# Top-32 attention and a hard-swish feed-forward in one kernel: attention in steps of two units, feed-forward blocks of 256 tokens

## The chip, the cores and the metric

The kernel runs on one core of one Trainium2 chip. The metric is the device time of one execution in microseconds (us). The engines are TensorE (PE in the rows; PEld is its weight load), VectorE (DVE), ScalarE (ACT), GpSimd (POOL) and SyncE (SP), which issues the DMAs here.

## The reference

`q`, `k` and `v` have 8 batches, 8 heads, 576 rows and 64 columns, in float32. For each head, scores are `q @ k.T / 8`. In each row the 32 largest scores stay, the others become -1e9; then a softmax with 1e-9 added to its denominator, and a product with `v`. The heads of a token, side by side, are a row of 512, so there are 4608 rows `x`. The feed-forward is

```
h = x @ w_in                      # 512 x 2048
g = h * clip(h + 3, 0, 6) / 6
out = g @ w_out                   # 2048 x 512
```

The two weight matrices arrive as 64-bit floats and are turned into float32 on the chip.

## The kernel before, in words

**Units.** A pair is two heads of one batch (four pairs in a batch, `Pair`). Its 576 rows of q and k are loaded, transposed on TensorE and copied out of PSUM once (`Pair.transpose`, L171 to L185). A unit is one pair and one tile of 128 query rows (`Unit`); the last 64 rows of both heads of a pair share a rest unit with half the work for DVE. A batch has 16 full and 4 rest units, and 160 units run in one loop (L448).

**A unit's steps.** `scores` (L198): matmuls into the PSUM tile `big`, two copies by ACT into `sc`. `top` (L228): four rounds, each a MAX8 for every row tile and, but for the last round, a MATCH_REPLACE8; this is nearly all of DVE's work. `exp` (L240): three small POOL instructions, then two passes of ACT over each row tile and an add on POOL. `weights` (L263): a reciprocal on DVE and a scaling of each row tile on POOL. `transpose` (L271): nine transposes (six for a rest unit) into `big`, one ACT copy to `eT`. `values` (L282): 20 matmul calls into a PSUM tile `pv`, and an ACT copy for two units together (L418).

**Buffers in PSUM.** `big` has one buffer of four banks, and scores, transposes and the transposes of q and k all go through it. `h`, `acc` and `pv` share four buffers of one bank (`ps_w`), and so does `f` of the weight conversion.

**Feed-forward.** When all four pairs of a token tile have their values, `queue` appends a `feed_forward` generator (L300). It takes 128 tokens in 16 pieces: 8 pieces for h (two pieces fill one `h` tile of four 128-column results, then ACT makes `g`, and a `gate` on DVE finishes it two pieces later), and 8 for the second product (L328). The loop asks for a number of pieces at set places (`piece`, L361); for a full unit four when `left`, the pieces still queued, is at least 8, and else three; for a rest unit two or one. After the loop all that is left runs (L503).

**Order.** The program is scheduled by hand: each engine's queue holds its instructions in the order in which the program lists them. In iteration n the loop lists the scores of unit n+1, the four rounds of unit n, `exp` of unit n-1, and weights, transposes and values of unit n-2. While n is under 8 the lag is one unit: weights, transposes and values are those of unit n-1 and come after round 2. Between the rounds stand four conversions of a weight chunk per unit (`convert`, L95), 32 in all, each with two ACT, two DVE and two POOL instructions.

Of the kernel before, what the change touches and what calls it, by code (L numbers as in the profile page):

```python
# [15 lines left out]
TOP_K = 32  # L16
# [11 lines left out]
def kernel(  # L28
# [26 lines left out]
    ldpool = pool("ld", 2)  # L55
# [10 lines left out]
    ps_w = pool("ps_w", 4, space=PSUM)  # L66
# [12 lines left out]

    ring = []  # L80
    for i in range(2 * NHP):
        vm = const([P, 2, J, D], f"vm{i}")
        vr = const([P, 2, D], f"vr{i}")
        nc.gpsimd.memset(vr[:], 0.0)
        ring.append((vm, vr))

    def big():

        return ps_big.tile([P, 4 * 512], F32, tag="big", name="big")
# [5 lines left out]
    def convert(dst, src):  # L95
# [10 lines left out]
        f = ps_w.tile([P, WC], F32, tag="w", name="f")  # L106
# [3 lines left out]
        nc.scalar.activation(f[:], lo, AF.Copy, bias=2.0, scale=2.0**-51)  # L110
# [7 lines left out]
            out=yu, in0=hi, scalar=0x80000000, in1=f[:].bitcast(U32),  # L118
# [18 lines left out]
    class Pair:  # L137


        def __init__(self, b, hp):  # L140
            self.b, self.hp = b, hp
            self.vm, self.vr = ring[(b * NHP + hp) % len(ring)]

        def load(self):
            h0 = 2 * self.hp
            self.rest = ldpool.tile([P, 2, D], F32, tag="rest", name="rest")
            for i, (name, src) in enumerate((("kin", k), ("qin", q))):
                t = ldpool.tile([P, J, 2, D], F32, tag=name, name=name)
                setattr(self, name, t)
                for hh in range(2):  # L150
                    nc.sync.dma_start(
                        t[:, :, hh, :],
                        src[self.b, h0 + hh, 0:JP, :].rearrange("(p j) d -> p j d", j=J),
                    )
                nc.sync.dma_start(
                    self.rest[i * R : (i + 1) * R, :, :],
# [14 lines left out]
        def transpose(self):  # L171
            kq = kqpool.tile([P, 2, S], F32, tag="kq", name="kq")
            self.kT, self.qT = kq[:, 0, :], kq[:, 1, :]
            ps = big()
            for i, src in enumerate((self.kin, self.qin)):
                for j in range(J):
                    rows = src[:, j, :, :].rearrange("p h d -> p (h d)")
                    c0 = i * JP + j * P
                    nc.tensor.transpose(ps[:, c0 : c0 + P], rows, ident[:])  # L179
            c0 = 2 * JP  # L180
            nc.tensor.transpose(
                ps[:, c0 : c0 + P], self.rest[:].rearrange("p h d -> p (h d)"), ident[:]
            )
            nc.scalar.copy(kq[:, :, 0:JP], ps[:, 0:c0].rearrange("p (t s) -> p t s", t=2))
            nc.scalar.copy(kq[:, :, JP:S], ps[:, c0 : c0 + P].rearrange("p (t s) -> p t s", t=2))  # L185

    class Unit:
# [5 lines left out]
        def __init__(self, pair, qt):  # L193
            self.pair, self.qt = pair, qt
            self.rest = qt == J
            self.nt = 1 if self.rest else 2

        def scores(self):  # L198
            pr, q0 = self.pair, self.qt * P
            ps = big()  # L200
            qs = slice(q0, min(q0 + P, S))
            heads = [slice(0, D), slice(D, P)]
            sc = self.sc = scpool.tile([P, 2 * (S + R)], F32, tag="sc", name="sc")
            if self.rest:
                for s0, s1 in ((0, JP), (JP, S)):
                    for d in heads:
                        nc.tensor.matmul(ps[d, s0:s1], pr.qT[d, qs], pr.kT[d, s0:s1])  # L207
                nc.gpsimd.memset(sc[:, S : S + R], 0.0)
                nc.scalar.copy(sc[:, 0:S], ps[:, 0:S])
                return  # L210
            banks = ps[:].rearrange("p (n s) -> p n s", s=512)
            for i, (s0, s1) in enumerate(((0, JP), (JP, S))):
                for hh, d in enumerate(heads):
                    nc.tensor.matmul(banks[:, 2 * i + hh, 0 : s1 - s0], pr.qT[d, qs], pr.kT[d, s0:s1])  # L214
            nc.scalar.copy(  # L215
                sc[:].rearrange("p (h s) -> p h s", h=2)[:, :, 0:JP], banks[:, 0:2, 0:JP]
            )
            nc.scalar.copy(  # L218
                sc[:, JP : JP + 2 * R].rearrange("p (h r) -> p h r", h=2), banks[:, 2:4, 0:R]
            )  # L220

        def begin(self):
            self.m = mpool.tile([P, 2, TOP_K], F32, tag="m", name="m")
            self.wk = wkpool.tile([P, 2, S], F32, tag="wk", name="wk")
            self.row = [self.sc[:, t * S : (t + 1) * S] for t in range(self.nt)]
            self.cur = list(self.row)

        def top(self, r):  # L228

            for t in range(self.nt):  # L230
# [9 lines left out]
        def exp(self):  # L240

            nt = self.nt
            kth = mpool.tile([P, 2], F32, tag="kth", name="kth")
            shift = mpool.tile([P, 2], F32, tag="shift", name="shift")
            self.den = mpool.tile([P, 2], F32, tag="den", name="den")
            last = self.m[:, 0:nt, TOP_K - 1]
            nc.gpsimd.tensor_scalar_mul(kth[:, 0:nt], last, -1.0)  # L247
            nc.gpsimd.tensor_tensor(shift[:, 0:nt], last, self.m[:, 0:nt, 0], ALU.subtract)
            nc.gpsimd.tensor_scalar_mul(shift[:, 0:nt], shift[:, 0:nt], scale)
            for t in range(nt):  # L250
                nc.scalar.activation(  # L251
                    self.row[t], self.row[t], AF.Prelu, bias=kth[:, t : t + 1], scale=1.0,
                    alpha=STEEP,
                )
            for t in range(nt):
                nc.scalar.activation(  # L256
# [283 lines left out]
```

## Time and profile before

| | us |
|---|---|
| median of 3 runs | 1802.66 (1802.39 to 1805.76) |
| the profiled execution, its own time | 1803.79 |
| span of its instructions | 1802.0 |
| PE busy | 1638.0 (91%) |
| DVE busy | 1548.2 (86%) |
| ACT busy | 968.7 (54%) |
| POOL busy | 408.3 (23%) |
| mean granted clock of TensorE | 0.970 |

The profile has 40 equal slices of 45 us. PE is at 3 to 8 tenths in the first five and at 9 in nearly all others; DVE is at 5 to 9 in the first eight, at 8 or 9 later, and at 2 and 0 in the last two. A matmul in float32 shows up as two instructions, so the counts of matmuls are twice those of the calls.

### The profile page before, as it was taken

The numbers are of one execution on the slowest core, as the hardware profiler recorded it, in microseconds if no ns is written. First come the engines' busy times: TensorE is split into PE (matmuls) and PEld (weight loads), VectorE is DVE, ScalarE is ACT, GpSimd is POOL, SyncE is SP. The second block draws the span as 40 slices with busy tenths as digits, with TensorE's granted clock in tenths as the row PEclk, the third lists the DMA queues.
The fourth block names the chain that finished last, engine by engine and source line by source line (L and its number), as shares of the span: only waits on it lengthen the run. The fifth ranks groups of instructions, "written<-read, shape, count | busy, mean of one in ns | idle before, by whom it ended". The sixth has DMA issues, their size and how long they took to land.

```text
span 1802.0 us, 31081 instructions
## 1 busy us (share of the span) xinstructions
PE 1638.0 (91%) x11872; PEld 1198.3 (66%) x11872; DVE 1548.2 (86%) x3249; ACT 968.7 (54%) x1717; POOL 408.3 (23%) x1038
## 2 busy tenths in 40 slices
PE   3356798989999999999999999999999999999999
PEld 2244666667677777777777766677677666777775
DVE  5767788989899899999999988999899888999920
ACT  5444555555655655555655555556555555555530
POOL 3544122222122112212121221211121122122110
PEclk9867899999999999999999999999999999999999
DMA  6431100011001110111011100011011010000000
GB/s 189 135 114 55 46 7 14 15 26 46 7 7 46 27 27 7 27 46 27 7 27 27 46 7 7 26 46 27 7 27 27 26 27 7 7 7 7 7 7 12
DMA packets 101140, 56.53 MB, mean 31 GB/s; under 512 B 84096, under 2 KB 92288, under 8 KB 100992
## 3 DMA queue, kind: packets, MB, share of 16 engines
q1 hardware_dynamic: 100992, 54.55, 10.9%
q8 instruction: 94, 1.54, 0.3%
q14 instruction: 54, 0.44, 0.1%
HBM read 45.09 MB, written 9.44 MB: 30 GB/s over the span
## 4 chain that ended last, share of the span: by engine, by line
PE 68%; ACT 15%; DVE 9%; issue 5%; POOL 2%; DMA 1%; SPq 0%; ACTq 0%
PE acc L328 22%; PE h L309 20%; PE pv L290 9%; PE big L214 8%; ACT sc L256 6%; DVE m L231 5%; PE big L278 5%; ACT eT L280 4%; DVE wk L235 4%; ACT sc L251 3%; PE big L179 2%; PE big L207 1%; DVE g L321 1%; DMA st<-in_moe_w_in_dram 1%; POOL a L108 1%
## 5 line engine op out<-in xcount | busy, mean ns | idle before, releaser
L231 DVE MAX8 m<-wk 128x8 f32<-128x576 f32 x864 | 614.5, 748 | 1.8
L328 PE MATMUL acc<-w_out,g 128*128 128x512 f32 x1152 | 540.6, 608 | 0.3 <-DVE g L321 0.3
L309 PE MATMUL h<-xT,w_in 128*128 128x128 f32 x4096 | 493.9, 278 | 0.0
L309 PEld LDWEIGHTS h<-xT,w_in 128*128 128x128 f32 x4096 | 474.5, 193 | 7.9 <-issue 3.3
L235 DVE MATCH_REPLACE8 wk<-m,wk 128x576 f32<-128x576 f32 x576 | 424.0, 743 | 0.0
L328 PEld LDWEIGHTS acc<-w_out,g 128*128 128x128 f32 x1152 | 208.6, 193 | 204.0 <-issue 194.9
L267 POOL TENSOR_SCALAR sc<-sc,den 128x576 f32<-128x576 f32 x288 | 213.4, 750 | 348.9 <-DVE den L265 337.9
L278 PE MATMUL big<-ident,sc 128*128 128x128 f32 x1344 | 181.0, 281 | 70.3 <-POOL sc L267 69.0
L231 DVE MAX8 m<-sc 128x8 f32<-128x576 f32 x288 | 203.9, 745 | 39.6 <-ACT sc L218 32.1
L278 PEld LDWEIGHTS big<-ident,sc 128*128 128x128 f32 x1344 | 160.7, 146 | 114.8 <-POOL sc L267 71.1
L261 POOL TENSOR_SCALAR den<-den 128x2 f32<-128x2 f32 (+1 forms) x160 | 35.2, 220 | 886.7 <-ACT sc L256 886.7
L256 ACT ACTIVATE sc<-sc,shift 128x576 f32<-128x576 f32 x288 | 219.8, 766 | 3.0
L251 ACT ACTIVATE sc<-sc,kth 128x576 f32<-128x576 f32 x288 | 209.0, 771 | 15.7 <-POOL kth L247 15.7
L321 DVE SCALAR_TENSOR_TENSOR g<-g,h 128x512 f32<-128x512 f32 x144 | 97.8, 679 | 137.4 <-ACT g L317 137.3
L214 PE MATMUL big<-kq 64*128 64x512 f32 (+1 forms) x1024 | 176.9, 467 | 42.5 <-ACT eT L280 29.2
L280 ACT COPY eT<-big 128x1152 f32<-128x1152 f32 (+1 forms) x160 | 167.0, 1044 | 86.7 <-PE big L278 86.2
L235 DVE MATCH_REPLACE8 wk<-m,sc 128x576 f32<-128x576 f32 x288 | 212.0, 743 | 0.0
L215 ACT COPY sc<-big 128x1024 f32<-128x1024 f32 x128 | 129.6, 1013 | 136.6 <-PE big L214 136.6
L317 ACT ACTIVATE g<-h,three 128x512 f32<-128x512 f32 x144 | 99.1, 688 | 186.9 <-PE h L309 185.4
L214 PEld LDWEIGHTS big<-kq 64*128 64x128 f32 x1024 | 92.9, 196 | 136.9 <-issue 77.5
L290 PE MATMUL pv<-eT,vm 128*64 128x128 f32 (+1 forms) x2560 | 163.9, 272 | 9.6 <-ACT eT L280 8.5
L290 PEld LDWEIGHTS pv<-eT,vm 128*64 128x64 f32 x2560 | 134.8, 140 | 52.4 <-issue 27.6
(43 smaller groups left out, 915.1 us busy)
## 6 DMA issues: line engine op xcount, KB each, us to landing
kin<-in_k_dram SPq DMA_DIRECT2D x64, 128.0 KB, 3.0
qin<-in_q_dram SPq DMA_DIRECT2D x64, 128.0 KB, 2.9
st<-in_moe_w_in_dram SPq DMA_DIRECT2D x16, 512.0 KB, 4.5
vm<-in_v_dram SPq DMA_DIRECT2D x64, 128.0 KB, 2.4
st<-in_moe_w_out_dram SPq DMA_DIRECT2D x16, 512.0 KB, 3.7
out_dram<-o SPq DMA_DIRECT2D x32, 256.0 KB, 2.3
rest<-in_k_dram SPq DMA_DIRECT2D x32, 32.0 KB, 2.5
rest<-in_q_dram SPq DMA_DIRECT2D x32, 32.0 KB, 2.6
```

Of the source, the lines that this page charges most:

```text
L214: nc.tensor.matmul(banks[:, 2 * i + hh, 0 : s1 - s0], pr.qT[d, qs], pr.kT[d, s0:s1])
L215: nc.scalar.copy(sc[:].rearrange("p (h s) -> p h s", h=2)[:, :, 0:JP], banks[:, 0:2, 0:JP])
L231: nc.vector.max(self.m[:, t, 8 * r : 8 * r + 8], self.cur[t])
L235: nc.vector.match_replace(wk, self.m[:, t, 8 * r : 8 * r + 8], self.cur[t], LOWEST)
L251: nc.scalar.activation(self.row[t], self.row[t], AF.Prelu, bias=kth[:, t : t + 1], scale=1.0, alpha=STEEP,)
L256: nc.scalar.activation(self.row[t], self.row[t], AF.Exp, bias=shift[:, t : t + 1], scale=scale, accum_out=self.den[:, t : t + 1],)
L267: nc.gpsimd.tensor_scalar(self.row[t], self.row[t], self.den[:, t : t + 1], 1.0, ALU.mult, ALU.mult)
L278: nc.tensor.transpose(ps[:, i * P : (i + 1) * P], self.sc[:, c0 : c0 + P], ident[:])
L280: nc.scalar.copy(eT[:, 0:n, :].rearrange("p c q -> p (c q)"), ps[:, 0 : n * P])
L290: nc.tensor.matmul(dst[hh * D : (hh + 1) * D, :], pr.vm[:, hh, c, :] if c < J else pr.vr[:, hh, :], rhs, start=(c == 0), stop=(c == J),)
L309: nc.tensor.matmul(h[:, (f - f0) * P : (f - f0 + 1) * P], w_in[:, i, f * P : (f + 1) * P], xT[:, i, :], start=(i == 0), stop=(i == NHP - 1),)
L328: nc.tensor.matmul(acc[:], gs[f // 4][:, (f % 4) * P : (f % 4 + 1) * P], w_out[:, f, :], start=(f == 0), stop=(f == NFC - 1),)
```

## The change

`Duo` takes the place of `Unit`: two pairs at the same query tile. A batch has eight full and two rest duos, 80 in all. In iteration m the program lists the second `exp` of duo m-1, the scores of duo m+1, eight rounds (four for the first unit of duo m, four for the second) with a conversion after each, and between them weights, transposes and values of duo m-1, and `exp` of the first unit of duo m after its round. The pieces are asked for at four places, six to eight for a full duo (with `left` under 10, under 20, or from 20) and two to four for a rest duo. There is no early phase with another lag.

`big` has five banks, `ps_w` three buffers. The last 64 columns of k are kept in a separate tile `kr` with zeros at the other head's place, so that one matmul over 128 rows gives them for both heads. One ACT copy takes the main part of four score banks (2048 columns), one takes 18 transposes (2304 columns). The conversion's `f` goes to SBUF, into `y`. Loads of q and k share the ring of nine buffers with the transposed tiles. `feed_forward` takes 128 or 256 tokens; with 256 the first product has 256 moving columns, and the second runs twice over the same `g`. Blocks of 256 hold two neighbouring query tiles, but for the first two tiles of the first batch, the last two of the last batch and the tiles of rest rows. The diff, cut:

```
-    kqpool = pool("kq", 2 * NHP)
-    scpool = pool("sc", 4)
-    wkpool = pool("wk", 2)
+    kqpool = pool("kq", 2 * NHP + 1)
+    scpool = pool("sc", 3)
+    wkpool = pool("wk", 1)
...
-    etpool = pool("et", 2)
+    etpool = pool("et", 1)
...
-    ps_w = pool("ps_w", 4, space=PSUM)
+    ps_w = pool("ps_w", 3, space=PSUM)
...
-        return ps_big.tile([P, 4 * 512], F32, tag="big", name="big")
+        return ps_big.tile([P, 5 * 512], F32, tag="big", name="big")
...
-        nc.scalar.activation(f[:], lo, AF.Copy, bias=2.0, scale=2.0**-51)
+        nc.scalar.activation(y[:], lo, AF.Copy, bias=2.0, scale=2.0**-51)
...
-            out=yu, in0=hi, scalar=0x80000000, in1=f[:].bitcast(U32),
+            out=yu, in0=hi, scalar=0x80000000, in1=yu,
...
# Pair.transpose
+            nc.scalar.copy(kq[:, 0:c0], ps[:, 0:c0])
+            nc.scalar.copy(kq[:, c0 : c0 + R], ps[:, c0 + R : c0 + 2 * R])
+            for hh in range(2):
+                d = slice(hh * D, (hh + 1) * D)
+                nc.scalar.copy(self.kr[d, hh, :], ps[d, c0 : c0 + R])
...
# Duo.scores, full duo
+            for i, u in enumerate(us):
+                pr = self.pairs[u]
+                for hh, d in enumerate(heads):
+                    nc.tensor.matmul(banks[:, 2 * i + hh, :], pr.qT[d, qs], pr.kT[d, :])
+            for i, u in enumerate(us):
+                pr = self.pairs[u]
+                nc.tensor.matmul(
+                    left[:, i * P : (i + 1) * P], pr.qT[:, qs], pr.kr[:].rearrange("p h r -> p (h r)")
+                )
...
# Duo.transpose
+            for u in range(2):
+                for c0 in starts:
+                    nc.tensor.transpose(
+                        ps[:, n * P : (n + 1) * P], self.sc[:, u, c0 : c0 + P], ident[:]
+                    )
+                    n += 1
             nc.scalar.copy(eT[:, 0:n, :].rearrange("p c q -> p (c q)"), ps[:, 0 : n * P])
...
# feed_forward
+        nf = 512 // nt
+        for f0 in range(0, NFC, nf):
             h = ps_w.tile([P, 512], F32, tag="w", name="h")
+            for f in range(f0, f0 + nf):
+                if f == f0 + nf // 2:
                     yield None
                 for i in range(NHP):
                     nc.tensor.matmul(
+                        h[:, (f - f0) * nt : (f - f0 + 1) * nt],
                         w_in[:, i, f * P : (f + 1) * P],
+                        xT[:, i, 0:nt],
...
+        for t0 in range(0, nt, P):
+            acc = ps_w.tile([P, DM], F32, tag="w", name="acc")
...
# the loop
+    for m in range(ND + 1):
...
+        if m:
+            prev.exp(1)
+        else:
+            first[2].transpose()
+            first[3].transpose()
+        if m + 1 < ND:
+            duos[m + 1].scores()
+        top(0)
+        piece(count[0])
...
+        top(1)
+        if m:
+            prev.weights()
+        piece(count[1])
+        top(2)
+        if m:
+            prev.transpose()
+        top(3)
+        if u:
+            u.exp(0)
...
+        piece(count[2])
+        top(4)
+        p = pair_at(m, 5)
+        if p:
+            p.transpose()
+        top(5)
+        piece(count[3])
+        top(6)
+        if m:
+            values(m - 1)
+        top(7)
+        if m == 2:
+            piece(3)
```

Here `top(r)` lists round r % 4 of unit r // 4 of duo m and then one conversion.

## Rows read from the trace of the kernel before

**Rows 1.** The page's first part: busy time, share of span, instructions.

```profile
PE 1638.0 (91%) x11872; PEld 1198.3 (66%) x11872; DVE 1548.2 (86%) x3249; ACT 968.7 (54%) x1717; POOL 408.3 (23%) x1038
```

**Rows 2.** By stage: PE, PEld, DVE, ACT, POOL busy us (count); clock, DMA, GB/s.

```profile
15.80:150.00 134.20, 57.09 (x351) 46.49 (x352) 102.25 (x203) 68.86 (x122) 68.42 (x93) 0.81 0.45 140
150.00:294.00 144.00, 121.30 (x825) 85.59 (x824) 119.26 (x250) 72.28 (x129) 33.51 (x83) 0.89 0.08 20
294.00:1721.30 1427.30, 1378.15 (x10238) 1010.68 (x10238) 1319.62 (x2784) 809.08 (x1439) 300.19 (x839) 0.99 0.08 22
1721.30:1802.00 80.70, 76.70 (x450) 52.67 (x447) 7.04 (x13) 13.71 (x22) 3.73 (x8) 0.99 0.03 11
```

**Rows 3.** The same stretches, MAX8 (L231) alone.

```profile
15.80:150.00 134.20, 38.22 (x54) 0.81 0.45 140
150.00:294.00 144.00, 62.52 (x89) 0.89 0.08 20
294.00:1721.30 1427.30, 705.81 (x1009) 0.99 0.08 22
```

**Rows 4.** Critical chain after 1741 us: start, duration, instructions merged.

```profile
1741.75 14.49 PE h L309 x128
1756.24 13.74 PE acc L328 x32
```

**Rows 5.** Timeline of PE, 902 to 916 us: start, duration, group.

```profile
902.04 1.09 PE L290 MATMUL pv<-eT,vm 128*64 128x128 f32 x16
...
904.37 1.30 PE L214 MATMUL big<-kq 64*128 64x512 f32 x8
905.60 3.70 PE L328 MATMUL acc<-w_out,g 128*128 128x512 f32 x8
909.14 1.15 PE L278 MATMUL big<-ident,sc 128*128 128x128 f32 x9
910.12 3.60 PE L328 MATMUL acc<-w_out,g 128*128 128x512 f32 x8
```

**Rows 6.** What PE waited for, 500 to 1700 us: total, times, longest.

```profile
PE big L214 <- ACT eT L280: 14.8, 16, 2.2
PE big L179 <- ACT eT L280: 11.3, 10, 1.9
```

**Rows 7.** Timeline of DVE around one unit's rounds.

```profile
899.87 1.41 DVE L231 MAX8 m<-sc 128x8 f32<-128x576 f32 x2
...
902.71 0.67 DVE L321 SCALAR_TENSOR_TENSOR g<-g,h 128x512 f32<-128x512 f32 x1
...
910.17 1.41 DVE L231 MAX8 m<-sc 128x8 f32<-128x576 f32 x2
```

**Rows 8.** What PE waited for in the first 150 us.

```profile
PE big L278 <- POOL sc L267: 61.3, 6, 11.4
```

**Rows 9.** Timeline of PE in the first 40 us.

```profile
12.16 2.40 PE L214 MATMUL big<-kq 64*128 64x512 f32 x8 [4.31 <-ACT kq L185]
```

**Rows 10.** Groups of ACT instructions by form: count, busy us, mean ns, idle before.

```profile
L280 ACT COPY eT<-big 128x1152 f32<-128x1152 f32 x128 | 141.8, 1108 | 79.4 <-PE big L278 78.9
L280 ACT COPY eT<-big 128x768 f32<-128x768 f32 x32 | 25.2, 788 | 7.3 <-PE big L278 7.2
L215 ACT COPY sc<-big 128x1024 f32<-128x1024 f32 x128 | 129.6, 1013 | 136.6 <-PE big L214 136.6
```

**Rows 11.** The two DVE lines of the conversion: ns min/median/max.

```profile
L116 DVE TENSOR_SCALAR a<-a x32: 402/417/1499, 18.6 to 163.3; 128x512 uint32<-128x512 uint32 x32
L117 DVE SCALAR_TENSOR_TENSOR y<-st,f x32: 667/675/686, 18.9 to 163.6; 128x512 uint32<-128x512 uint32 x32
```

**Rows 12.** Timeline of all engines, 906 to 914 us: one unit's exp, another's weights.

```profile
906.78 1.45 ACT L251 ACTIVATE sc<-sc,kth 128x576 f32<-128x576 f32 x2
...
909.82 0.22 POOL L261 TENSOR_SCALAR den<-den 128x2 f32<-128x2 f32 x1 [4.73 <-ACT sc L256]
913.27 1.47 POOL L267 TENSOR_SCALAR sc<-sc,den 128x576 f32<-128x576 f32 x2 [3.23 <-DVE den L265]
```

More of the change, by code (lines that the diff above doesn't have):

```diff
@@ L171, in transpose @@
         def transpose(self):
-            kq = kqpool.tile([P, 2, S], F32, tag="kq", name="kq")
-            self.kT, self.qT = kq[:, 0, :], kq[:, 1, :]
+            kq = kqpool.tile([P, JP + S], F32, tag="kq", name="kq")
+            self.kT, self.qT = kq[:, 0:JP], kq[:, JP : JP + S]
             ps = big()
[L175 to L179, printed above, removed]
@@ L180, in transpose @@
-            c0 = 2 * JP
[L181 to L194, printed above, removed]
+            for j in range(2 * J + 1):
+                rows = self.landed[:, j, :, :].rearrange("p h d -> p (h d)")
+                nc.tensor.transpose(ps[:, j * P : (j + 1) * P], rows, ident[:])
@@ L220, in scores, with row, top @@
             )
[L222 to L228, printed above, removed]
+        def row(self, u, t):
+            return self.sc[:, u, t * S : (t + 1) * S]
+        def top(self, u, r):
+            if r == 0:
+                self.m = mpool.tile([P, 2, TOP_K], F32, tag="m", name="m")
+                self.wk = wkpool.tile([P, 2, S], F32, tag="wk", name="wk")
+                self.cur = [self.row(u, t) for t in range(self.nt)]
@@ L376, in piece, with queue, values, rows @@
                     gate()
+    def queue(*block):
+        nonlocal left
+        todo.append(feed_forward(*block))
+        left += block[1] // 8
+    state = {}
+    def values(m):
+        u = duos[m]
+        b, qt, hp = u.pairs[0].b, u.qt, u.pairs[0].hp
+        if u.rest:
+            if b % 2 == 0 and hp == 0:
+                state["xr"] = xrpool.tile([P, NHP, P], F32, tag="xr", name="xr")
+            u.values(state["xr"][:, hp : hp + 2, (b % 2) * R : (b % 2 + 1) * R])
+            if b % 2 == 1 and hp == 2:
+                def rows(t0):
+                    return [
+                        (i * R, (i + 1) * R, out[(b - 1 + i) * S + JP : (b + i) * S, :])
+                        for i in range(2)
+                    ]
+                queue(state["xr"], P, rows)
+            return
+        two = not (b == 0 and qt < 2 or b == B - 1 and qt >= 2)
+        c0 = qt % 2 * P if two else 0
+        if hp == 0 and c0 == 0:
+            state["xT"] = xtpool.tile([P, NHP, 2 * P], F32, tag="xT", name="xT")
+        u.values(state["xT"][:, hp : hp + 2, c0 : c0 + P])
+        if hp == 2 and (not two or c0):
+            def rows(t0):
+                t = qt - c0 // P + t0 // P
+                return [(0, P, out[b * S + t : b * S + JP : J, :])]
+            queue(state["xT"], c0 + P, rows)
     chunks = list(weight_chunks())
@@ L381, in convert_step @@
     def convert_step(depth=1):
-        if converting and (len(converting) > depth or not chunks):
+        while len(converting) > depth:
+            next(converting.pop(0), None)
+        if converting and not chunks:
             next(converting.pop(0), None)
@@ new lines, in pair_at, with top @@
+    def pair_at(m, first):
+        b, at = divmod(m, per_batch)
+        return pairs[b + 1][at - first] if b + 1 < B and 0 <= at - first < NHP else None
+    first = pairs[0]
+    first[0].load()
+    convert_step(2)
+    first[0].transpose()
+    duos[0].scores((0,))
+    first[1].load()
+    convert_step(2)
+    first[1].transpose()
+    duos[0].scores((1,))
+    first[2].load()
+    convert_step(2)
+    first[3].load()
+    for m in range(ND + 1):
+        u = duos[m] if m < ND else None
+        prev = duos[m - 1] if m else None
+        level = (left >= 10) + (left >= 20)
+        if u and u.rest:
+            count = [(1, 0, 1, 0), (1, 0, 1, 1), (1, 1, 1, 1)][level]
+        else:
+            count = [(2, 1, 2, 1), (2, 2, 2, 1), (2, 2, 2, 2)][level]
+        depth = 2 if m < 2 else 1
+        def top(r):
+            if u:
+                u.top(r // 4, r % 4)
+            convert_step(depth)
+        if m:
+            prev.exp(1)
+        else:
+            first[2].transpose()
[4 more added lines that the diff above has]
+        piece(count[0])
+        p = pair_at(m, 3)
```

283 lines of the change are left out of this document (100 added, 183 removed).

## The prediction

> **What bounds the kernel now.** I read the page's busy times first [rows 1]: PE 1638.0 of 1802.0 us, DVE 1548.2. Both are near the span, so the stages decide. I cut the span where the MAX8s of a batch end, 144 to a batch [rows 2, 3].
>
> From 294 to 1721 us seven batches run, 203.9 us each; PE is busy 1378.15 of 1427.3 us (97%), DVE 92%, at a granted clock of 0.99. This stage is bound by PE, with DVE close behind. After the last MAX8 80.7 us of almost pure PE work remain. The first batch takes 294 us: at its start 54 MAX8s run in 134 us against 71 in 100 later, PE is busy 57 us of 134, and its wait there is for scaled weights, 61.3 us in six waits [rows 2, 3, 8]. There the lag of one unit binds: exp, weights, transposes and values of one unit are done before the next one's exp.
>
> **Unit costs.** A 128-token block costs 14.49 us for h (128 instructions, 0.113 each) and 13.73 to the next start for acc (32, 0.429 each); a piece is 28.2/16 = 1.76 us [rows 4]. For a full unit, from start to next start: scores 1.23, transposes 0.98, values 2.33 for two units with the switch behind them. Eight acc instructions ahead of the transposes take 3.54, not 8 x 0.429 = 3.43, so a switch is 0.1; with two of them a unit costs 3.6 us [rows 5]. A rest unit I put at 2.5 us (six of nine transposes, half the columns in values) and a pair's nine transposes at 1.1. A batch so holds 16 x 3.6 + 4 x 2.5 + 4 x 1.1 = 72 us of attention on PE.
>
> DVE takes 10.30 us from one unit's first MAX8 to the next one's, with one gate of 0.67, so 9.63 for rounds and reciprocal [rows 7]; a full duo 19.3.
>
> **The change part by part.**
>
> *Fewer weight loads.* 28 of 36 token tiles get 256 moving columns. On the line through the two paces above, 256 columns cost 0.113 + (0.429 - 0.113)/3 = 0.218 us, against 2 x 0.113: 64 such instructions a tile save 0.5 us, 28 tiles 14 us. Bounds: nothing, or 20 if the time per column fell to that of 512 columns. The loads are already hidden: PEld's 1198 us lie beside PE's 1638 in a span of 1802 [rows 1]. Gates, Relus and output DMAs stay as many.
>
> *Duos on PE.* The 512-column scores of two units stay; eight 64-column instructions become four of 128 columns over both heads, about even. Eighteen transposes and 40 calls of values now follow each other, so half the switches go: 0.3 us a duo, 19 us over 64. Bounds: 0, and 38 if each start saves twice that.
>
> *ACT.* The two lengths of the eT copy give 0.83 ns a column and 150 ns an instruction [rows 10]: 2304 columns take 2.07 us instead of two of 1.11, 2048 score columns 1.85 instead of two of 1.01. Two more copies of 64 columns per pair, 0.2 each, are 13 us over 64. ACT is free 46% of the span [rows 1], which hides them; uncovered they cost those 13 us.
>
> *Buffers.* All scores and transposes still pass one `big`. Before, PE waited for it 26 us in 1200, 4.4 a batch [rows 6]. Now each copy is twice as long and comes half as often, and 3.5 to 7 us of pieces stand between scores and transposes, and between transposes and the next scores. I laid one full duo against DVE's time, zero at its first round. The second exp of the duo before ends 3.3 after DVE's last round [rows 12]; ACT's scores copies follow to 5.7; DVE's reciprocal stands at 5.6; POOL scales four row tiles in 2.94, to 8.8; PE, with scores (2.5) and four pieces (7.0) first, wants them at 9.5 and 10.5. So PE need not wait unless it runs a microsecond ahead. Behind that ACT does eT to 13.8, the next exp to 16.8, then the third Relu, whose gate stands on DVE at 17: if PE is late by 1 us, DVE waits 1 us. The three `ps_w` buffers suffice here (the third h wants one at 11.5, the first gate frees it at 6.8). With four gates DVE needs 21.8, without any 19.4, PE 20.7 in both. I take the 4.4 us of idle a batch that PE had; bounds 1 (all absorbed) and 10 (1 us a duo). Fewer `sc`, `et` and `wk` buffers cost nothing: a buffer is wanted a duo after its last reader. The fourth pair's load may wait for a buffer of transposed k and q that is read until a duo later; values and output stores stand behind it on SP, all wanted a duo later or more, so this is hidden too; without that cover it is 3 us of a load per batch.
>
> *Work moved to the end.* By the code, the first batch now runs 36 pieces (before 48), the loop 524 in all (544), and 52 (32) remain after it. No work is added, but DVE is idle longer at the end.
>
> *The start.* PE starts the first scores at 12.2 and takes 2.40 us, not 1.30 as later [rows 5, 9], so at half pace, 1.2 and not 2.4 GHz. On that pace scores and copies of the first unit reach 16, where DVE starts; transposes and copies of pair 1 20, its scores 24, pairs 2 and 3 31, scores of duo 1 39. Only then ACT gets to the fourth weight chunk, which DVE wants after three rounds and a MAX8 round with three conversions, at 29: 12 us lost. A conversion takes DVE 1.0 to 1.1 us [rows 11]. So duo 0 ends near 55, duo 1 near 83, the rest duo, with 8 us of waits for exp and for chunks behind the eT copy, near 110, duo 3 near 143 (before, this work ended near 150). Six more duos with few pieces take 5 x 21.2 + 11 + 8 of waits: 268 against 294. Bounds: 250 (no waits) and 294.
>
> One more cost can fall on this path. L116 takes 0.41 us mostly and up to 1.50; L117 took 0.67 to 0.69 always, with one input in PSUM [rows 11]; now both its inputs are in SBUF. If it waited, like L116, for a POOL scaling (0.73 each [rows 12]) half of the time, as POOL is busy half of this stage [rows 2], 32 instructions would lose 12 us; I count nothing, as its own row shows no spread. The Trainium skill, "SBUF — State Buffer", Who interferes with whom, says that a DVE instruction with two SBUF inputs contends with GpSimd instructions that read SBUF; the trace has no such DVE instruction to show it, and by that rule the sum below would be 12 us higher.
>
> **The sum.** Span: first batch 268. Seven batches of loop: 480 pieces at 1.74 (835), attention 7 x (72 - 2.4) (487), idle 7 x 4.4 (31), the missing hundredth of the clock (13): 1366. After the loop 60 pieces at 1.76 (106) and 5 us of values and last output: 111. Together 1745. Before, by the same terms, a batch was 69.7 pieces (123), 72 of attention and 9 of idle and clock. The profiled execution took 1.8 us more than its span and 1.1 more than the median, so the median should be **1745** too.
>
> **Rivals.**
>
> *No waits:* the loop runs at PE's pace and the start at its lower bound: 250 + 835 + 487 + 13 + 111 = 1696. For it: in the layout DVE and PE nearly balance. Against: the tight Relu, and rest duos, where PE has 14 us and DVE 10.
>
> *Loads were not hidden:* if loads set the pace of h, halving them on 28 tiles saves 28 x 64 x 0.113 = 202 us, and the time is 1745 - 202 + 14 = 1557. Against: 0.88 ns a column at 128 and 0.84 at 512 [rows 4] leave no room for that. The Trainium skill, "TensorE: Matmul & The Clock Gate", Back-to-back issue gap, has 81 ns for 128 columns and 131 for 512, by which wide matmuls would be far cheaper per column; these rows don't agree.
>
> *The start gains nothing* and idle stays at 9: 294 + 835 + 487 + 63 + 111 = 1790.
>
> *No change:* the start's waits grow by what the loop saves, 1799 to 1806.
>
> *Slower: PE waits for `big`.* One buffer of five banks, emptied by a 2.07 us copy in ACT's queue. If in each of 80 duos PE stood through that copy before it may write again, it would be 1745 + 166 = 1911; through half of it 1828. It decides from 0.8 us a duo on (61 us over 80). For it: this is PE's main wait in the steady stage [rows 6], and where PE idled the clock was 0.81 and 0.89 [rows 2]. Against: more pieces stand in between. The Trainium skill, "Perfetto Trace Analysis", Optimizing Tensor Performance, wants independent groups to rotate through PSUM banks so that one's evacuation overlaps the next one's matmuls, which speaks against one large tile.
>
> **Numbers.** Forecast (1710 to 1780) 0.57; no waits 0.12; loads not hidden 0.01; start gains nothing (1780 to 1799) 0.13; no change 0.04; slower 0.13. A measurement can tell about 0.2% (3.6 us). Faster 0.83, same 0.04, slower 0.13. For 8 in 10 the range reaches from 1690, with most of the fast case, to 1800, with the gainless start but not the slow case.
>
> **What would show it.** After: 144 MAX8s by about 268 us, then some 195 us per batch with PE at 97%, then about 110 us of PE alone; h instructions 0.218 us apart; PE's waits for the eT copy under 30 us in 1200. The prediction is wrong if those waits, or DVE's for Relu, come to over 1 us a duo, or if the first batch still takes 290 us.

## The result, and the profile after

The changed kernel takes 1737.36 us in the median (1736.34 to 1738.36), the kernel before 1802.53 in the runs beside it: ratio 0.9635, 95% interval [0.9618, 0.9651]. The forecast was 1745. The profiled execution took 1738.36 us with a span of 1736.6. The page's first part answers to [rows 1]:

```profile
PE 1607.3 (93%) x9824; PEld 1111.1 (64%) x9824; DVE 1544.7 (89%) x3169; ACT 947.1 (55%) x1559; POOL 413.8 (24%) x1030
```

DVE's work is the same to 4 us. PE is busy 30.7 us less; the other 34.7 of the span's 65.4 us were PE's idle time. The table of busy times by stage, cut again at the starts of the 144th and the last MAX8, answers to [rows 2]:

```profile
16.10:150.50 134.40, 70.93 (x413) 50.86 (x413) 114.78 (x211) 75.87 (x130) 81.00 (x102) 0.75 0.47 144
150.50:260.30 109.80, 86.00 (x620) 63.68 (x622) 109.46 (x231) 66.29 (x112) 25.91 (x71) 0.86 0.12 31
260.30:1622.20 1361.90, 1334.66 (x8178) 918.88 (x8176) 1311.17 (x2715) 782.94 (x1282) 299.57 (x826) 0.99 0.08 21
1622.20:1736.60 114.40, 110.50 (x608) 75.03 (x603) 9.23 (x15) 16.92 (x26) 3.71 (x8) 1.00 0.04 12
```

The same stretches for MAX8 (L247) alone, as in [rows 3]:

```profile
16.10:150.50 134.40, 39.46 (x56) 0.75 0.47 144
150.50:260.30 109.80, 60.86 (x89) 0.86 0.12 31
260.30:1622.20 1361.90, 707.15 (x1009) 0.99 0.08 21
```

The first batch ends at 260.3 us (before 294, forecast 268), the seven others take 1361.9 (before 1427.3, forecast 1366), and 114.4 remain (before 80.7, forecast 111): -33.7, -65.4 and +33.7. Part of this is work that moved from stage to stage: by the counts of h and acc instructions in the traces, the first batch now runs 32 pieces (before 45), the loop 484 (491) and the rest 60 (40). At 1.76 us a piece, 13 of the loop's 65 us are work that now runs after it.

In the loop PE is busy 98% and DVE 96%. What DVE waited for in the loop of the kernel before:

```profile
DVE g L321 <- ACT g L317: 61.6, 46, 3.0
DVE den L265 <- POOL den L261: 20.5, 23, 3.4
DVE m L231 <- ACT sc L218: 15.0, 12, 2.3
DVE m L231 <- ACT sc L209: 5.9, 3, 3.7
```

and in the loop of the changed kernel:

```profile
DVE g L352 <- ACT g L348: 35.2, 18, 4.2
DVE den L281 <- POOL den L277: 10.4, 16, 1.6
```

103 us of waits have become 46. DVE's work in this stretch went down by 8.5 us (1319.6 to 1311.2: 70 reciprocals less). So 57 of the loop's 65 us are, seen from DVE, waits that are gone: the scores are always there in time (21 us), the Relu is late 18 times and not 46, the denominators half as long. Seen from PE, it is 43.5 us less busy and 22 less idle (49.1 to 27.2). Of the 43.5 us, 13 are the wide h (priced below), 13 the pieces that moved behind the loop and 3 the clock (0.994 for 0.992); some 15 are left for the step of two units. What PE waited for in the loop, beside [rows 6]:

```profile
PE big L298 <- POOL sc L285: 18.2, 14, 5.8
PE big L176 <- ACT eT L302: 2.7, 6, 0.5
PE pv L316 <- ACT eT L302: 2.2, 1, 2.2
```

The wait for the eT copy is all but gone; what is left is for POOL's scaled weights. PE's timeline, as in [rows 5]:

```profile
901.77 6.17 PE L361 MATMUL acc<-w_out,g 128*128 128x512 f32 x14
907.78 1.47 PE L298 MATMUL big<-ident,sc 128*128 128x128 f32 x12
909.09 7.07 PE L340 MATMUL h<-xT,w_in 128*128 128x256 f32 x32
...
917.40 1.99 PE L224 MATMUL big<-kq 64*128 64x512 f32 x8
919.32 0.71 PE L227 MATMUL big<-kr,kq 128*128 128x128 f32 x4
919.87 7.07 PE L340 MATMUL h<-xT,w_in 128*128 128x256 f32 x32
926.78 2.33 PE L298 MATMUL big<-ident,sc 128*128 128x128 f32 x18
```

From start to start, 32 h instructions of 256 columns take 6.91 us, 0.216 each, and 14 acc instructions 6.01, 0.429 each, also where transposes follow. At the start DVE's timeline has the forecast stall, 10.4 us for POOL's (and before it ACT's) part of the fourth weight chunk:

```profile
27.22 1.41 DVE L247 MAX8 m<-wk 128x8 f32<-128x576 f32 x2
39.03 1.49 DVE L117 TENSOR_SCALAR a<-a 128x512 uint32<-128x512 uint32 x1 [10.39 <-POOL a L109]
```

### The profile page after: what moved, and what is told of

Read it like the earlier page. It is cut to its first block, busy times and chain, and to the rows that moved or that the text cites. A ratio compares the mean times of both kernels' runs of the same rounds, so it can differ in the third digit from the quotient of the medians.

```text
span 1736.6 us, 26566 instructions
## 1 busy us (share of the span) xinstructions
PE 1607.3 (93%) x9824; PEld 1111.1 (64%) x9824; DVE 1544.7 (89%) x3169; ACT 947.1 (55%) x1559; POOL 413.8 (24%) x1030
## 4 chain that ended last, share of the span: by engine, by line
DVE 50%; PE 38%; ACT 5%; POOL 4%; issue 2%; SPq 0%; DMA 0%; ACTq 0%; POOLq 0%
DVE m L247 25%; DVE wk L251 20%; PE acc L361 16%; PE h L340 8%; PE pv L316 4%; PE big L298 4%; DVE g L352 3%; PE big L224 3%; POOL sc L285 2%; ACT sc L272 1%; PE big L176 1%; ACT eT L302 1%; PE big L227 1%; PE big L212 1%; DVE y L118 1%
## 5 line engine op out<-in xcount | busy, mean ns | idle before, releaser
L247 DVE MAX8 m<-wk 128x8 f32<-128x576 f32 x864 | 614.8, 749 | 2.3
L361 PE MATMUL acc<-w_out,g 128*128 128x512 f32 x1152 | 513.0, 594 | 0.0
L340 PE MATMUL h<-xT,w_in 128*128 128x256 f32 (+1 forms) x2304 | 462.6, 358 | 2.6 <-ACT xT L323 2.6
L340 PEld LDWEIGHTS h<-xT,w_in 128*128 128x128 f32 x2304 | 395.6, 192 | 49.1 <-issue 4.0
L361 PEld LDWEIGHTS acc<-w_out,g 128*128 128x128 f32 x1152 | 212.2, 191 | 230.0 <-issue 228.1
L302 ACT COPY eT<-big 128x2304 f32<-128x2304 f32 (+1 forms) x80 | 156.2, 1952 | 231.0 <-PE big L298 231.0
L298 PE MATMUL big<-ident,sc 128*128 128x128 f32 x1344 | 191.2, 292 | 88.4 <-POOL sc L285 84.7
L247 DVE MAX8 m<-sc 128x8 f32<-128x576 f32 x288 | 204.0, 746 | 15.2 <-ACT sc L233 15.2
L262 POOL TENSOR_SCALAR kth<-m 128x2 f32<-128x2 f32 (+1 forms) x160 | 36.0, 225 | 472.5 <-DVE m L247 471.4
L224 PE MATMUL big<-kq 64*128 64x512 f32 x512 | 131.6, 633 | 7.4 <-ACT kr L182 7.4
L230 ACT COPY sc<-big 128x2048 f32<-128x2048 f32 (+1 forms) x65 | 118.6, 1824 | 20.0 <-PE big L227 20.0
```

Of the source, the lines that this page charges most:

```text
L224: nc.tensor.matmul(banks[:, 2 * i + hh, :], pr.qT[d, qs], pr.kT[d, :])
L247: nc.vector.max(self.m[:, t, 8 * r : 8 * r + 8], self.cur[t])
L298: nc.tensor.transpose(ps[:, n * P : (n + 1) * P], self.sc[:, u, c0 : c0 + P], ident[:])
L302: nc.scalar.copy(eT[:, 0:n, :].rearrange("p c q -> p (c q)"), ps[:, 0 : n * P])
L340: nc.tensor.matmul(h[:, (f - f0) * nt : (f - f0 + 1) * nt], w_in[:, i, f * P : (f + 1) * P], xT[:, i, 0:nt], start=(i == 0), stop=(i == NH ...
L361: nc.tensor.matmul(acc[:], gs[f // nf][:, c0 : c0 + P], w_out[:, f, :], start=(f == 0), stop=(f == NFC - 1),)
```

## The experiments

Each kernel was timed beside the kernel before on the same chip; the table goes by these ratios. "To the changed one" is the difference of its ratio to 0.9635, times 1802.5. The stages are cut at the ends of the 144th (in the third row 149th) and the last MAX8.

| kernel | median us | ratio [interval] | to the changed one | first batch, loop, rest |
|---|---|---|---|---|
| before | 1802.5 | 1 | +66 | 294.8, 1427.2, 80.0 |
| changed | 1737.4 | 0.9635 [0.9618, 0.9651] | 0 | 261.0, 1362.0, 113.6 |
| changed, one MAX8 more in 40 duos | 1746.3 | 0.9691 [0.9678, 0.9705] | +10 | 261.9, 1370.1, 113.7 |
| changed, more scores on PE | 1769.4 | 0.9814 [0.9801, 0.9828] | +32 | 266.7, 1387.5, 113.6 |
| changed, narrow h | 1741.0 | 0.9644 [0.9630, 0.9659] | +2 | 262.0, 1365.2, 111.7 |
| changed, both runs split | 1791.3 | 0.9924 [0.9909, 0.9939] | +52 | 261.2, 1413.5, 113.5 |
| changed, values split | 1751.6 | 0.9720 [0.9707, 0.9733] | +15 | 259.8, 1376.5, 113.3 |
| changed, no cover | 2113.8 | 1.1696 [1.1673, 1.1719] | +372 | 279.8, 1712.5, 120.0 |
| changed, start reordered | 1726.9 | 0.9567 [0.9553, 0.9581] | -12 | 250.9, 1362.1, 112.9 |
| the same, first batch in 128 | 1729.9 | 0.9577 [0.9561, 0.9592] | -10 | 256.4, 1358.2, 113.5 |
| the same, f in PSUM | 1735.8 | 0.9631 [0.9618, 0.9644] | -1 | 259.1, 1361.9, 113.6 |
| before, lag two | 1762.9 | 0.9775 [0.9753, 0.9797] | +25 | 257.0, 1424.1, 79.9 |
| before, blocks of 256 | 1819.6 | 1.0071 [1.0055, 1.0088] | +79 | 287.0, 1425.6, 105.7 |
| before, lag two and blocks of 256 | 1781.5 | 0.9862 [0.9845, 0.9879] | +41 | 248.3, 1425.4, 105.5 |

**The lag at the start.** The kernel before without its early phase:

```
-    EARLY = 8
+    EARLY = 0
```

> The kernel before with the early phase taken out: the lag of two units and the late place of weights hold from the first unit. Theory 1 (the lag of one unit bound the first batch): PE's wait for scaled weights in the first 150 us falls from 61 us to under 25, the first batch ends 20 to 30 us earlier (294 to about 270), and the time falls by 15 to 30 us, to 1773 to 1788. Rival (the conversions and the clock bound the first batch, whatever the lag): the first batch ends within 6 us of 294 and the time stays within 6 us of 1802.5.

It is 41 us faster, more than the 15 to 30 expected, nearly all of it in the first batch (294.8 to 257.0). PE's wait for scaled weights in the first 150 us, 61.3 in [rows 8], is here

```profile
PE big L278 <- POOL sc L267: 17.7, 4, 9.2
```

The changed kernel's first batch, 261.0, is no shorter than this, though 13 fewer pieces run in it. So the change gains no more there than the lag alone gives, which could be had without duos.

**Blocks of 256 tokens.** First in the changed kernel, the blocks as they are, but h in instructions of 128 columns:

```
-                for i in range(NHP):
...
+                for t in range(0, nt, P):
+                    c = (f - f0) * nt + t
+                    for i in range(NHP):
+                        nc.tensor.matmul(
+                            h[:, c : c + P],
+                            w_in[:, i, f * P : (f + 1) * P],
+                            xT[:, i, t : t + P],
```

> The changed kernel, with the blocks of 256 tokens and their order in the queue kept, but each first product of 256 columns issued as two of 128 with the weights loaded for each. It puts back the weight loads alone. Theory 1 (loads hidden, a small fixed cost per instruction): PE has 28 x 64 x (0.226 - 0.216) = 18 us more work at the paces of the two traces (0.113 per 128 columns, 6.91 us for 32 instructions of 256); the loop is bound by PE at 98%, so the time rises by 12 to 18 us, to 1749 to 1755. Rival A (the loads set the pace of h): the gain of the change lies here, +65 us and back near 1800. Rival B (DVE binds the loop now, PE's extra work falls into waits): under 4 us.

2 us by the ratios, 3.7 by the medians: no more than the intervals are wide, and on the side of Rival B. In this run's trace 64 narrow instructions take 7.15 us ahead of transposes, from start to start, and in the changed kernel 32 wide ones 6.91:

```profile
922.70 7.31 PE L342 MATMUL h<-xT,w_in 128*128 128x128 f32 x64
929.85 2.13 PE L298 MATMUL big<-ident,sc 128*128 128x128 f32 x18
```

The wide form so saves PE 0.95 us a block, 13 in all 14 blocks; the time shows 2 to 4 us of this. That the hidden loads mattered (+65) is out.

Then the blocks alone, in the kernel before (`feed_forward`, `queue` and the rows as in the change):

```
-    wkpool = pool("wk", 2)
+    wkpool = pool("wk", 1)
...
+            two = not (b == 0 and u.qt < 2 or b == B - 1 and u.qt >= 2)
+            c0 = u.qt % 2 * P if two else 0
...
+                queue(state["xT"], c0 + P, rows)
```

> The kernel before, with one change: feed-forward blocks of 256 tokens for the same 28 tiles (one buffer of wk instead of two makes room). Units, order and early phase stay. Theory: before, PE sets the loop's pace, so the PE work that wide blocks save (28 x 0.5 = 14 us) shows for the most part: 8 to 14 us faster, 1789 to 1795. Rival A, after the run in which the changed kernel with narrow instructions lost only 3.7 us: what PE saves is mostly waited away for exp, Relu and POOL, under 4 us. Rival B: blocks come in lumps of 32 pieces, so PE lacks work at times and more pieces (46 instead of 32 by the code) are left for the end: 0 to 15 us slower.

12.8 us slower: the rival of the lumps. The rest after the last MAX8 grows from 80.0 to 105.7, which is the 14 pieces at 1.76 that the code leaves for the end; the first batch, with 13 pieces fewer, gives 8 back, and the loop, with all 14 blocks of cheaper h in it, only 1.6. PE is busy 8.3 us less in this loop (1369.8 for 1378.1) but idle 6.7 more (55.8 for 49.1), and its clock is 0.985 for 0.992. And both, with `EARLY = 0`:

> The kernel before with a lag of two units from the start and with blocks of 256 tokens: everything of the change but the step of two units on TensorE. Theory: the parts add up, so 40 us from the lag and what the run with wide blocks alone gives: 1749 to 1763. What is then missing to 1737 is the duo's own share, 12 to 26 us (my estimate for half of the switches was 19). Rival: the duo order gives nothing itself, 1737 to 1742.

The blocks cost 16 us here too, so the time lies above the 1749 to 1763 expected. What remains to the changed kernel is 41 us, not 12 to 26. It is the step of two units together with what came along and was not run apart: the new order of the list, the five-bank `big`, three `ps_w` buffers, `kr`, and the conversion's `f` in SBUF. The loop takes 1362.0 us with it and 1425.4 without (10 of the 63 us are six pieces that move behind the loop); the first batch is 12.7 longer with it, of which 10.4 are the stall shown above, and the rest 8 longer. In this kernel's loop DVE waited for

```profile
DVE g L325 <- ACT g L321: 46.8, 35, 4.8
DVE den L265 <- POOL den L261: 27.6, 27, 3.6
DVE m L231 <- ACT sc L218: 23.4, 15, 3.4
DVE m L231 <- ACT sc L209: 2.9, 1, 2.9
```

101 us, as before. The step of two units, with what came along, takes 55 of these away.

**The runs on PE.** The changed kernel with a piece moved between the two units' transposes, and one between their values:

```
             for u in range(2):
...
+                if u == 0:
+                    piece(mid)
...
+        mid = min(count[1], 1) if m else 0
+        piece(count[1] - mid)
...
-            prev.transpose()
+            prev.transpose(mid)
...
+        mid = min(count[3], 1) if m else 0
+        piece(count[3] - mid)
```

> The changed kernel with one feed-forward piece put between the two units' transposes and one between their values, taken from the pieces that stood before them, so that the two tiles no longer follow each other in these two steps. Theory 1 (each change of step costs PE 0.1 us, the loop is bound by PE): four more changes a duo, 0.4 us, about 80 duos less the early ones, +15 to +26 us, 1752 to 1763. Rival A (the changes are free or hidden): within 4 us of 1737. Rival B (the transposes of the first tile start earlier against the scaling on POOL, and the eT copy ends later): PE's wait for POOL falls below the 18 us of the steady stage, its wait for the eT copy rises above 10 us, and the time moves by less than 10 us either way.

52 us, outside all three ranges and twice what more switches could cost. PE's timeline of this kernel shows the other half:

```profile
906.87 0.71 PE L227 MATMUL big<-kr,kq 128*128 128x128 f32 x4
907.42 1.88 PE L365 MATMUL acc<-w_out,g 128*128 128x512 f32 x4
911.32 2.12 PE L298 MATMUL big<-ident,sc 128*128 128x128 f32 x9 [2.02 <-POOL sc L285]
913.23 2.66 PE L365 MATMUL acc<-w_out,g 128*128 128x512 f32 x4
915.73 1.15 PE L298 MATMUL big<-ident,sc 128*128 128x128 f32 x9
916.71 1.88 PE L365 MATMUL acc<-w_out,g 128*128 128x512 f32 x4
```

The piece that went between the transposes is missing ahead of them, and PE stands there 2.02 us for POOL's weights. Over the loop this wait is 47.5 us in 36 times (18.2 in 14), and DVE's waits are 94.6 us (45.6). The values' split alone, to tell the halves apart:

> The changed kernel with a piece between the two units' values only (the transposes stay together). In the run with both splits PE's switches cost little, but the copy of the values to xT stands ahead of the next duo's exp in ACT's queue, and a piece (1.74 us) now delays it. Theory (late copy, late exp, late reciprocal on DVE): most of that run's 54 us, 30 to 55: 1767 to 1792, and DVE's waits for the denominators up from 10 to 30 us in the loop. Rival (the split transposes, by a late copy of eT, were the cause): under 15 us, below 1753.

15 us, and DVE waits 60 us. My theory of the late copy ahead of exp falls with this. PE's own work explains the 15 us:

```profile
901.45 1.98 PE L363 MATMUL acc<-w_out,g 128*128 128x512 f32 x4
903.37 1.09 PE L316 MATMUL pv<-eT,vm 128*64 128x128 f32 x16
```

The four acc instructions between the values take 1.92 us and not 1.72. Sixteen acc and the values of a duo take 6.96 and 2.33 us in the changed kernel; split they take 5.25, 1.24, 1.91 and 1.24, so 0.35 more a duo and 22 in 64. In the loop PE is busy 15.5 us longer and idle as long as before (26.3 for 27.2).

About 37 us are left, by difference, for the split transposes, which were not run alone. Two things changed there at once: a piece is missing ahead of the first nine, and the eT copy comes a piece later. PE's wait for POOL's weights grew by 29 us and its waits for the eT copy by under 4, which speaks for the first, but no run separates them.

**The cover.** All pieces that stand between scores and transposes, moved behind the transposes:

```
         top(0)
-        piece(count[0])
...
-        piece(count[1])
         top(2)
         if m:
             prev.transpose()
+        piece(count[0])
         top(3)
         if u:
             u.exp(0)
+        piece(count[1])
```

> The changed kernel, with the pieces that stand between a duo's scores and the transposes of the duo before listed after the transposes. No work is added. Theory (the pieces hide the way from scores over exp and POOL's scaling to the transposes): PE stands before the transposes in 72 duos by 3 to 6 us, and what comes later on PE (values, their copy ahead of the next exp in ACT's queue) is late too, so 1.5 to 3.5 us a duo: 1850 to 1990. Rival (the engines shift against each other and take the wait up elsewhere): under 20 us, below 1757.

372 us, 4.7 a duo, above the range, and no work added. Of the loop's 350 us more, PE is idle 269 (295.8 for 27.2) and busy 82 longer (1416.8 for 1334.7) at a clock of 0.92 for 0.99. The waits of PE and of DVE in this loop:

```profile
PE big L298 <- POOL sc L285: 246.3, 51, 10.1
PE big L298 <- ACT sc L233: 46.0, 19, 2.9
```

```profile
DVE g L352 <- ACT g L348: 242.0, 67, 7.5
DVE den L281 <- POOL den L277: 148.3, 34, 9.5
```

So a slower order of duos is real, though by another wait than the slower rival's: PE waits for POOL's weights, hardly for `big`. The forecast put the turning point at 0.8 us a duo, and this order is far beyond. What keeps the change on the good side is the place of the three or four pieces between scores and transposes: with one of them moved between the transposes (and with split values) it costs 52 us, with all behind the transposes 372. The moved pieces take their Relus along, behind the eT copy and an exp in ACT's queue, and DVE waits 242 us for them; how much of the 372 is PE's missing cover and how much the Relus' place was not run apart.

**Who sets the pace of the changed loop.** One more MAX8 in every second duo:

```
+            if u == 0 and r == 0 and self.pairs[0].hp == 0:
+                nc.vector.max(spare[:], self.cur[0])
```

> The changed kernel plus one MAX8 into a spare tile at the first round of every second duo (those of the first two pairs): 40 x 0.75 = 30 us more work on DVE, nothing else. Theory (the loop of the changed kernel goes at the pace of DVE's work plus its waits for exp and Relu): nearly all of it shows, 22 to 31 us, 1759 to 1768. Rival (PE, 98% busy, sets the loop, and DVE's 51 us of idle take the extra work in): 0 to 12 us, below 1750.

One score matmul more in each full duo:

```
-                for hh, d in enumerate(heads):
+                for hh, d in [(0, heads[0]), (1, heads[1]), (1, heads[1])][: 3 - i]:
```

> The changed kernel with one of the four 512-column score matmuls of a full duo issued twice (same result in the same bank): 64 x 0.48 = 31 us more work on PE, 27 of it in the loop, which has 27 us of PE idle. Theory (DVE's work and waits set the pace; 13 us more PE work cost 3.7 in the run with narrow instructions): the same share of it shows, 7 to 15 us, 1744 to 1753. Rival (PE sets the pace): 25 to 31 us, 1762 to 1769.

The first cost 10 us: the rival's side. But the MAX8 were less work than I had counted, 0.66 us each to the next start, 26 in all (DVE's busy time rose by 25.3):

```profile
902.02 0.74 DVE L248 MAX8 spare<-sc 128x8 f32<-128x576 f32 x1
902.68 1.40 DVE L250 MAX8 m<-sc 128x8 f32<-128x576 f32 x2
```

The second cost 32, and here more was put in than I had counted: in this kernel's timeline the ten score instructions take 2.77 us from start to start, eight of them 1.92 in the changed kernel, so 0.86 more a duo and 55 in all.

```profile
914.87 2.85 PE L224 MATMUL big<-kq 64*128 64x512 f32 x10
917.64 0.71 PE L227 MATMUL big<-kr,kq 128*128 128x128 f32 x4
```

A microsecond of work so costs 0.4 us on DVE and 0.6 on PE at this place, and 0.7 on PE with split values (15 for 22), against 0.1 to 0.3 for the narrow h. The profile page of each run has the chain of work that ended last, followed back through the whole span. Here are those of the kernel before, of the changed one, and of the one with more scores on PE:

```profile
PE 68%; ACT 15%; DVE 9%; issue 5%; POOL 2%; DMA 1%; SPq 0%; ACTq 0%
```

```profile
DVE 50%; PE 38%; ACT 5%; POOL 4%; issue 2%; SPq 0%; DMA 0%; ACTq 0%; POOLq 0%
```

```profile
PE 65%; DVE 28%; ACT 2%; POOL 2%; issue 1%; DMA 1%; SPq 1%; ACTq 0%; POOLq 0%
```

The change moved half of the chain from PE to DVE, and 55 us more on PE moved it back. The chain names one path and not how close the next one is: 26 us more on the engine that leads it cost only 10. Neither engine is the bound alone: PE's idle time takes a small load in, and a large one runs into DVE's waits (71 us for Relu and denominators in this run's loop, 46 in the changed kernel's). The theory that nearly all of DVE's added work shows falls.

**The start.** In the first duo, transposes of pairs 2 and 3 behind the first two rounds, and the scores of duo 1 behind the fourth:

```
-        else:
-            first[2].transpose()
-            first[3].transpose()
-        if m + 1 < ND:
+        if m and m + 1 < ND:
             duos[m + 1].scores()
         top(0)
+        if m == 0:
+            first[2].transpose()
...
         top(1)
+        if m == 0:
+            first[3].transpose()
...
         top(3)
+        if m == 0:
+            duos[1].scores()
```

> The changed kernel with, in the first duo, the transposes of pairs 2 and 3 listed after the first and the second round and the scores of duo 1 after the fourth, in place of all three ahead of the first round. Theory 1 (the fourth chunk's conversion is late because ACT comes to it only after those copies): DVE's wait of 10.4 us at 28 us of the span is gone, the first batch ends 8 to 12 us earlier, and the time falls by as much, to 1726 to 1730. Rival (the wait moves to a later chunk, or the loop, bound by PE, gives the time back since pieces come no earlier): under 4 us.

The first batch ends at 250.9, 10.1 us earlier, and all else stays: the 10.4 us stall is given back whole. This is the fastest kernel of the study, 12 us below the changed one by the ratios and 10 by the medians. On top of it, blocks of 128 for all of the first batch:

```
-        two = not (b == 0 and qt < 2 or b == B - 1 and qt >= 2)
+        two = not (b == 0 or b == B - 1 and qt >= 2)
```

> The changed kernel with the start reordered as in the run before (10.4 us faster) and all tiles of the first batch as blocks of 128 tokens, so that pieces are there earlier: by the code 8 pieces more run in the first ten duos and 8 fewer in the next ten, and 52 stay for the end. Theory (PE has room in the first batch, and DVE, at 186 of 192 us, sets the second): 0 to 5 us beyond the reordered start, 1722 to 1727. Rival (PE sets the second batch): 8 x 1.74 = 14 us beyond it, 1713.

Nothing that the intervals can tell: the first batch is 5.5 us longer, the second 3.7 shorter (188.1 for 191.8). And with the conversion's f in PSUM again:

```
+        f = ps_w.tile([P, WC], F32, tag="w", name="f")
...
-        nc.scalar.activation(y[:], lo, AF.Copy, bias=2.0, scale=2.0**-51)
+        nc.scalar.activation(f[:], lo, AF.Copy, bias=2.0, scale=2.0**-51)
...
-            out=yu, in0=hi, scalar=0x80000000, in1=yu,
+            out=yu, in0=hi, scalar=0x80000000, in1=f[:].bitcast(U32),
```

> The changed kernel with the reordered start (which ran 10.4 us faster than the changed kernel) and the conversion's f back in PSUM. Theory (the conversion's second DVE instruction waits for GpSimd when both inputs lie in SBUF: mean 0.84 against 0.68 us, 32 of them, 5 us, all in DVE-bound first duos): 2 to 5 us beyond the reordered start, 1722 to 1725. Rival (f takes one of three PSUM buffers that h, acc and pv want in the first batch): nothing or some us slower, 1727 to 1735.

The conversion's second DVE instruction, in the run with the reordered start and then in this one (count, busy us, mean ns):

```profile
L118 DVE SCALAR_TENSOR_TENSOR y<-st,y 128x512 uint32<-128x512 uint32 x32 | 27.2, 851 | 0.0
```

```profile
L119 DVE SCALAR_TENSOR_TENSOR y<-st,f 128x512 uint32<-128x512 uint32 x32 | 21.7, 677 | 3.3 <-POOL w_out L123 3.0 <-ACT f L112 0.3
```

So 5.5 us of DVE's time do come back, but the kernel is 11.5 us slower by the ratios and 9 by the medians. In this run pv waits for a buffer that the conversion holds, the rival's mechanism, though PE's waits in the first 260 us are 93 us in all as against 96 with the reordered start, since those for weights are shorter. DVE's waits from its first round on go from 9 to 23 us there; that the late pv is what brings these about is argued and not shown. One of PE's waits in that stretch:

```profile
PE pv L317 <- DVE y L119: 27.8, 3, 13.3
```

## Why the prediction was right, and where not

**The sum.** Every stage came within 8 us: first batch 260.3 for 268, a batch of the loop 194.6 for 195, the rest 114.4 for 111. PE's idle in the loop was put at 31 us and was 27. In the first batch the near hit is partly luck, and in the loop the sum took PE's saved work for saved time, which the runs do not bear out.

**What bounds the loop.** "Bound by PE, with DVE close behind" named one engine where the two hold each other up. Less PE work did not help by itself: 13 us less for h gave 1.6 in the loop before and 2 to 4 in the changed kernel. The loop's gain is there only with the step of two units, and with it 57 us of DVE's waits and 22 of PE's are gone. How the gain divides between switches saved, hand-overs saved and the parts that came along isn't settled: no run changed the one without the others.

**Wide blocks.** The duration was right (0.218 forecast, 0.216 measured), the 14 us on PE too (13); that they show in the time was the step that failed. Blocks alone are a loss, 12.8 us, since a block of 32 pieces comes late and leaves more for the end: the term "work moved to the end", which I had counted in the sum without laying it at their door. The changed kernel with blocks of 128 throughout was not run.

**Switches.** The 0.1 us was put at the wrong place. In [rows 5] the run of 3.54 us follows scores; 14 acc instructions that lead into transposes take 6.01, 0.429 each, and nine transposes between pieces 0.98, 0.109 each, in the run with both splits (915.73 to 916.71). Around transposes a switch costs nothing. Where scores or values border on pieces it is 0.1: the four kr instructions between scores and pieces take 0.55 and not 4 x 0.11, and 16 acc instructions ahead of values 6.96 (median of 11 such runs) and not 6.87. By that a duo saves one change into scores and one out of them, 0.2 us and 13 in all, not 19; the 15 us left in PE's account of the loop fit this. The prediction also counted the values, but those of two units stood together before too (40 instructions, which are 20 calls, in 2.33 us). The Trainium skill, "TensorEngine Tiling (Array Packing)", Key Properties, says that a change of the tiling mode drains the engine: the trace agrees in so far as scores use 64 rows, values 64 columns, and pieces and transposes the full array, and a change costs 0.1 us here and nothing is lost around transposes; a drain itself stands in no row.

**The start.** The gain came from the lag, as the prediction said of [rows 8], and the run with the lag alone gives 41 us. The forecast 12 us stall measured 10.4, and the reordered start gave it back. Two errors cancel in part in the first batch: its first four duos ended at 150.8 us and not at 143, and the six after them took 110 us and not the 125 that I had laid out with 8 us of waits. That the first scores ran at half pace stands in their duration (2.40 us for 1.30); the granted clock of that stretch, 12.16 to 14.60 us, reads 1.00, so the 1.2 GHz that I gave for it is not shown.

**Copies and buffers.** The eT copy took 2.08 us (2.07), the score copy 1.85 (1.85), the kr copies 0.21; in the loop all stayed hidden. PE's listed waits are 24 us in 1362, and DVE's for Relu 0.5 us a duo: both under the limits set. The slower rival named the wrong wait: even without cover PE waits 246 us for POOL's scaling and only 46 for score copies to free `big`, and DVE waits longer still (390 us for Relu and denominators).

**The two inputs in SBUF.** Counted at nothing, measured at 5.3 us in the changed kernel: 32 times 842 ns in the mean instead of 676. It comes in steps: 21 of the 32 took 0.67 to 0.69 us as before, ten 1.09 and one 1.75. The line in the changed kernel, beside [rows 11]:

```profile
L118 DVE SCALAR_TENSOR_TENSOR y<-st,y 128x512 uint32<-128x512 uint32 x32 | 27.0, 842 | 0.0
```

The Trainium skill, "SBUF — State Buffer", Who interferes with whom, was the better guide: two SBUF inputs contend with GpSimd's reads. The pair of runs above agrees, 851 ns with y in SBUF and 677 with f in PSUM; my estimate of 12 us by that rule was twice too high.

## What to carry to other kernels

Between an engine's hand-over and the point where it needs the answer, list enough independent work in that engine's own queue, and look at what that work waits for on its way: the same pieces listed behind the transposes cost 372 us. When two engines are both over 95% busy, an engine's saved work is worth a fraction of itself, so price it by adding a load to each engine, and measure in the trace how large that load came out. Take a change of several parts apart: here the lag gave 41 us, the larger blocks lost 16, the step of two units with its buffers and order gave 41, and a reordered start, which was not in it, 10 to 12 more.

## What the runs showed of the hardware

Score matmuls of 64 rows run in pairs: the two heads of a pair lie in different halves of the rows, their instructions start 7 ns apart in the trace, and four of 512 columns take 1.92 us. A fifth, left without a partner, added 0.86, as much as a pair. And a wait on PE can cost more than its own length. In the run without cover PE stood for 2.6 us until 911.08, and the eighteen transposes after that took 3.48 us from start to start instead of 1.97; two stretches of that run, the transposes and a later one, with the granted clock as the first number after the busy times:

```profile
911.10:914.50 3.40, 3.33 (x18) 3.02 (x19) 3.40 (x8) 0.00 (x0) 2.25 (x4) 0.65 0.00 0
926.40:929.90 3.50, 3.50 (x18) 2.82 (x16) 3.50 (x8) 1.43 (x4) 0.00 (x0) 1.00 0.02 5
```

The clock is 0.65 over the transposes, so for most of them at 1.2 and not 2.4 GHz, and 1.00 where PE had been busy before; over this kernel's loop it is 0.92, in the changed one's 0.99.
